# An attention and long-convolution kernel on one core: its instruction order planned with one more rule on PSUM banks

## The chip, the core and the metric

The kernel runs on one core of a Trainium2 chip. The metric is the device time of one execution in microseconds (us), the median of three runs. A core has five engines that run side by side, each in its own fixed order: TensorE (PE in the profile, its weight loads PEld), VectorE (DVE), ScalarE (ACT), GpSimd (POOL), and SyncE (SP), which here only starts transfers (DMA). Matrix products land in PSUM, which has eight banks of 512 float32 per partition; all other tiles lie in SBUF.

## The reference

Block-sparse attention, then a gated long convolution on its output. Four batches, eight heads, 768 positions, head size 64, model width 512.

```python
# attention, per batch and head
k_rep = k.reshape(B, H, 12, 64, D).mean(axis=3)          # mean key of each block of 64
gate_scores = einsum('bhsd,bhnd->bhsn', q, k_rep)        # blocks of the future: -1e9
top_idx = argsort(gate_scores)[..., -3:]                 # three best blocks, and the own one
scores = where(mask & causal, q @ k.T / sqrt(D), -1e9)
attn = softmax(scores) @ v
# hyena, per batch, x = heads side by side (768 x 512)
x1, x2, x3 = split(x @ w_proj, 3)
x2_conv = irfft(rfft(x2) * rfft(filter_fft))             # along the 768 positions
out = (x1 * x2_conv * x3) @ w_out
```

## The kernel before

The kernel works on 16 pairs of heads (`g` = 0 to 15, four pairs to a batch). Its work is first written down as a graph of 1509 small operations. Each has a tag, the engines that may run it with an assumed duration, the buffers it reads and writes, and a priority `vt`. A planner inside the kernel's source goes through the graph with a clock of its own, gives each operation an engine, a start and buffers, and sorts all operations by start. They are emitted in that order, and the framework adds the semaphores. It also makes two instructions of different engines that touch the same PSUM bank wait for each other in the order in which they were emitted.

The planner's parameters are one dictionary: offsets `v_tag` to the priority of each kind of operation, `d_tag` a handicap of VectorE where another engine may do it, `tm` the first pair whose queries are turned by DMA, `ahead` how far the planner may run in front of the attention, `warm_until` until when idle TensorE is filled with warm-up matmuls.

```python
PAR = dict(
    p0=-2.503, p1=0.149, a0=0.0, pvlag=0.364, dlag=1.728, dlen=1.178, ...
    o1=1.0, pen_dve=-0.346, ahead=3.319, delta=0.028, queue=6.537, direct=2, tm=8, kin=16, late=2.0,
    w0=1.334, wl=1.579, wlag=0.085, warm_until=31.758, tr0=-4.639, trl=2.112, fill0=-0.29, ...
)
```

The keys of a pair are transposed by TensorE into a PSUM bank, half by half. VectorE sums the bank to block means (`ks`), ScalarE or VectorE copies it to the key tile (`k2`). GpSimd splits the means into a high and a low part for the gate (`km`).

```python
def e_kt(...):  nc.tensor.transpose(E.bk(kp)[:, P*c:P*(c+1)], E.sb(kn[g])[:, HC*hf + c, :, :], E.id32)   # L368, 3 per half
def e_ks(...):  nc.vector.reduce_sum(E.sb(ks)[:, 6*hf:6*hf+6], E.bk(kp)[:, 0:HS]...)                    # L371
def e_k2(...):  (nc.scalar.copy if en == "ACT" else nc.vector.tensor_copy)(                             # L381, twice per half
                    E.sb(Kt[g])[r, HC*hf:HC*(hf+1), 1-t, :], E.bk(kp)[r, 0:HS]...)
...
def e_km(E, nc, en):
    for t in range(2):
        ...
        nc.gpsimd.tensor_copy(x[r, 2, 0:12], E.sb(ks)[r, :])                                            # L398
        nc.gpsimd.tensor_tensor(x[ru, 1, cc], E.sb(ks)[r, :], x[r, 2, 0:12], op=ALU.subtract)           # L399
        nc.gpsimd.tensor_copy(x[ru, 0, cc], x[r, 2, 0:12])                                              # L400
```

Queries take one of two ways. For pairs below `tm` TensorE transposes them (L430), ScalarE and VectorE split them (L433, L436), and after the gate (L488), the choice of blocks on VectorE (L507, L514) and a mask transpose (L536) the mask rows are copied in (L543). For pairs from `tm` on, the split is done before the turn (L458, L463), and two transposing DMAs (L468, L472) bring queries and masks to the query tile.

Attention: scores (L566), exp on ScalarE (L573), causal corner on GpSimd (L578), values (L596), normalising on VectorE (L605, L609), even and odd sums `eo` (L634, GpSimd or VectorE), a transposing DMA to `xT` (L628), and a first Fourier stage (L646, L653) copied to `XT` (L659, ScalarE or VectorE).

Hyena of a batch: products with the filter's spectrum `t` (L755, then L764 on VectorE), their sums `Y` (L774, GpSimd or VectorE), the two gates `x1` and `prod` (L791; L797 on ScalarE or VectorE, L800 on VectorE), the way back (L818), `ce` and `sd` (L827, L833), `yT` (L839, GpSimd or VectorE), output product (L849), eviction `osb` (L853, ScalarE or VectorE) and store (L856).

The planner's choice of the start of an operation and its bookkeeping, cut:

```python
def at(o, e, f):
    est = max(free[e], o.ready, f)
    if o.lock and e == "DVE":
        est = max(est, free["POOL"])
    if e == "POOL":
        est = max(est, lock_dve)
    if o.size > 200:
        est = max(est, chan - par["queue"])
    return est
...
    if e == "PE" and 0.4 <= free[e] < par["warm_until"] and (
            not cands or min(c[0] for c in cands) > free[e] + 0.1):
        cands.append((free[e], filler()))          # a warm-up matmul, L950 in the profile
```

Of the kernel before, what the change touches and what calls it, by code (L numbers as in the profile page):

```python
# [12 lines left out]
ALU = mybir.AluOpType  # L13
# [31 lines left out]
for _pi, _segs in enumerate(PIECES):  # L45
# [3 lines left out]


PAR = dict(
    p0=-2.503, p1=0.149, a0=0.0, pvlag=0.364, dlag=1.728, dlen=1.178, h0=5.163, hlen=3.776, f0=-0.278,
    f1=4.952, ld=-1.045, s2a=-0.184, s2b=0.461, x0=0.517, x1=0.943, c0=0.51, c1=0.761, o0=1.574,
    o1=1.0, pen_dve=-0.346, ahead=3.319, delta=0.028, queue=6.537, direct=2, tm=8, kin=16, late=2.0,
    w0=1.334, wl=1.579, wlag=0.085, warm_until=31.758, tr0=-4.639, trl=2.112, fill0=-0.29, v_yT=0.58, v_sd=0.159,
    d_k2=0.711, v_trig=-0.056, v_ldq=-0.072, v_max=0.214, v_g=1.014, v_Y=0.003, v_k2=-0.006, v_rec=-0.068, v_small=0.756,
    v_gate=-0.111, v_km=-0.109, d_x1=0.207, d_shQ=0.303, v_xT=-0.322, v_prod=-0.4, v_ldv=-0.291, d_yT=0.059, v_ks=0.021,
    v_osb=0.119, v_ldk=-0.647, v_kT=-0.152, v_gT=0.375, d_md=0.183, d_trig=0.402, v_qT=-0.009, v_mT=-0.03, v_lt=-0.053,
    v_fe=-0.62, d_eo=0.463, v_md=0.013, v_phase=0.942, v_shQ=0.405, v_ldf=0.502, d_Y=0.618, v_sel=-0.073, v_warm0=-0.481,
    v_x1=-0.19, v_ldw=-0.109, v_tab=-0.895, v_va=0.322, v_iota=0.312, d_XT=0.43, v_qh=0.06, v_h0=0.127, v_eblk=-1.554,  # L60
    v_id32=-0.347, v_st=0.292, v_nyq=0.459, v_s2=0.435, v_st1=0.097, v_XT=0.005, v_t=-0.034, v_ql=0.179, v_hf=0.099,
    d_g=0.166, d_ce=0.66, d_osb=-0.651, d_fill=0.096, v_w=-0.194, v_ce=-0.772, v_fill=-0.313, v_op=-0.002, v_pv=-0.131,
    d_w=0.06, v_nrm=-0.309, v_ha=-0.507, v_id16=-0.192, v_eo=0.145, v_x13=-0.234, d_fe=0.294, v_cv=0.151, v_sc=-0.043,
    v_T2=0.596, v_T1=0.196, d_qh=0.116, v_pq=-0.067, d_pq=0.376, v_ex=-0.001,
)

POOLS = dict(kn=2, qn=3, vn=2, k2=1, qx=4, ks=2, km=3, m8=2, nm=1,
# [8 lines left out]
class Buf:  # L76
    def __init__(self, pool, seq=None):
        self.pool, self.slot, self.left, self.seq = pool, None, 0, seq
        self.w, self.r = {}, {}
        self.free = self.busy = 0.0  # L80
        self.users = []


class Op:
# [4 lines left out]
class Graph:  # L89
# [3 lines left out]
    def add(self, tag, vt, eng, emit, rd=(), wr=(), res=(), lock=False, size=0):  # L93
        o = Op()
        vt += self.par.get("v_" + tag, 0.0)
        o.i, o.tag, o.vt, o.eng, o.emit, o.lock, o.size = len(self.ops), tag, vt, eng, emit, lock, size
        deps = set()

        def norm(xs):
            return [x if isinstance(x, tuple) else (x, 0) for x in xs]  # L100

        bufs = []
        for b, p in norm(rd):
            deps.update(b.w.get(p, ()))
            b.r.setdefault(p, []).append(o)
            bufs.append(b)
        for b, p in norm(wr):
            deps.update(x for x in b.w.get(p, ()))
            deps.update(x for x in b.r.get(p, ()) if x is not o)
            b.w.setdefault(p, []).append(o)  # L110
            bufs.append(b)
        deps.discard(o)
        o.deps = list(deps)
        o.bufs = list({id(b): b for b in bufs}.values())
        for b in o.bufs:
            b.left += 1
        o.alloc = list({id(b): b for b in o.bufs + list(res)}.values())
        self.ops.append(o)
        return o
# [17 lines left out]
def pol(occ):  # L137
    return occ, occ + 0.11


def build(par):
# [62 lines left out]
    def e_eblk(E, nc, en, h=0):  # L204
        x = E.eblk[64 * h:64 * h + 64, :]
        nc.gpsimd.memset(x, EMASK)
        nc.gpsimd.affine_select(out=x, in_=x, compare_op=ALU.is_ge, fill=0.0, base=0, pattern=[[1, S]],
                                channel_multiplier=-64)
        nc.gpsimd.affine_select(out=x, in_=x, compare_op=ALU.is_ge, fill=0.0, base=63, pattern=[[-1, S]],
                                channel_multiplier=64)  # L210

    for h in range(2):
        add("eblk", T0 + 3 + h, {"POOL": pol(2.2)}, lambda E, nc, en, h=h: e_eblk(E, nc, en, h), wr=[(cb("eblk"), h)])

    slot_init = []
    for i in range(POOLS["kt"]):
        def e_fq(E, nc, en, i=i):
            eng = nc.vector if en == "DVE" else nc.gpsimd
            eng.memset(E.t["qt"][i][0:64, :, 0, :], 0.0)
            eng.memset(E.t["qt"][i][64:76, 0, 1, :], 0.0)  # L220

        def e_fk(E, nc, en, i=i):
            eng = nc.vector if en == "DVE" else nc.gpsimd
            for h in range(2):
                r = slice(0, 64) if h == 0 else slice(64, 76)
                eng.tensor_copy(E.t["kt"][i][r, :, h, :], E.eblk[r, :].rearrange("p (c s) -> p c s", s=P))

        slot_init.append([
            add("fill", par["fill0"] + i, {"DVE": (0.55, 0.7), "POOL": pol(1.1)}, e_fq, wr=[cb(("slot", i))], lock=True),
            add("fill", par["fill0"] + i, {"DVE": (0.55, 0.7), "POOL": pol(1.6)}, e_fk,  # L230
                rd=[(cb("eblk"), 0), (cb("eblk"), 1)], wr=[(cb(("slot", i)), 1)], lock=True)])
    def e_small(E, nc, en):
        for t_ in E.t["km"]:
# [112 lines left out]
    def prep(g):  # L346
# [44 lines left out]
        def e_km(E, nc, en):  # L391
            x = E.sb(km)
            for t in range(2):
                r = slice(64 * t, 64 * t + 64)
                u = 1 - t if by_dma else t
                ru = slice(64 * u, 64 * u + 64)
                cc = slice(12 * u, 12 * u + 12)
                nc.gpsimd.tensor_copy(x[r, 2, 0:12], E.sb(ks)[r, :])  # L398
                nc.gpsimd.tensor_tensor(x[ru, 1, cc], E.sb(ks)[r, :], x[r, 2, 0:12], op=ALU.subtract)  # L399
                nc.gpsimd.tensor_copy(x[ru, 0, cc], x[r, 2, 0:12])  # L400

        add("km", v(.3), {"POOL": pol(1.45)}, e_km, rd=[(ks, 0), (ks, 1), cb("small")], wr=[km])

        def shuffle(src, col, dst, vt, tag):
            for t in range(2):
                def e_sh(E, nc, en, t=t):
                    r = slice(64 * t, 64 * t + 64)
                    o = E.sb(dst)[r, :, 1 - t, :]
                    i_ = E.sb(src)[r, col:col + S].rearrange("p (c s) -> p c s", s=P)
                    if en == "SP":  # L410
                        nc.sync.dma_start(o, i_)
                    else:
                        (nc.vector if en == "DVE" else nc.gpsimd).tensor_copy(o, i_)
                eng = {"DVE": dve(S, 4), "POOL": pol(0.86)} if direct else {"SP": (0.5, 0)}
                add(tag, vt, eng, e_sh, rd=[(src, 0), (src, 1)], wr=[(dst, ("h", t, 0)), (dst, ("h", t, 1))],
                    size=0 if direct else 130, lock=direct)

# [462 lines left out]
def plan(par):  # L880
# [81 lines left out]
# [5 lines that stand above are left out]
            est = max(est, lock_dve)  # L967
        if o.size > 200:
            est = max(est, chan - par["queue"])
        return est  # L970

    vt_floor = [o.vt for o in ops if o.tag == "sc"]
# [5 lines left out]
    while left:  # L978
# [29 lines left out]
        for b in o.alloc:  # L1008
            if b.pool is None or b.slot is not None:
                continue  # L1010
            s, f = slot_for(b)
            b.slot, b.free = s, f
            if b.seq is not None:
                turn[b.pool].remove(b.seq)
            kk = [("bk", i) for i in range(s, s + (2 if b.pool == "sp" else 1))] if b.pool in ("bk", "sp") else [(b.pool, s)]
            o.pre += [u for x in kk for u in last.get(x, ())]
            for x in kk:
                last[x] = b.users
            if b.pool in ("bk", "sp"):
                for i in range(s, s + (2 if b.pool == "sp" else 1)):  # L1020
                    banks[i] = None
            else:
                pools[b.pool][s] = None
# [26 lines left out]
        for s in o.succ:  # L1050
            s.ready = max(s.ready, o.done)
            s.nd -= 1
            if s.nd == 0:
                for x in s.eng:
                    ready[x].append(s)
        for b in o.bufs:
            b.left -= 1
            b.busy = max(b.busy, o.done)
            b.users.append(o)
            if b.left == 0 and b.pool is not None:  # L1060
                if b.pool in ("bk", "sp"):
                    for i in range(b.slot, b.slot + (2 if b.pool == "sp" else 1)):
                        banks[i] = b.busy
                else:
                    pools[b.pool][b.slot] = b.busy
# [91 lines left out]
```

## Time and profile before

| | |
|---|---|
| median time, three runs | 246.58 us (246.48 to 246.77) |
| span of the profiled run | 245.2 us |
| PE busy | 229.1 us, of it 17.2 warm-up matmuls (114) |
| DVE busy | 207.7 us, 642 instructions |
| ACT busy | 171.5 us, 287 instructions |
| POOL busy | 151.2 us, 304 instructions |
| mean DMA rate | 169 GB/s |

The span is a little shorter than the time, since it runs from the first to the last instruction. Busy time counts an engine while it works on an instruction; matmuls are pipelined and their ends are modelled, so TensorE can be called busy and still have small gaps. A line such as "ACT kt L381 <- DVE ks L371" in the view of waits says that ScalarE stood idle before line 381 until VectorE had done line 371; the engine that gave the last signal is named.

### The profile page before, as it was taken

The page shows a single profiled execution, that of the slowest core. Times are in us where ns is not written, and L with a number is a line of the kernel's source. Part 1 is how long each engine was busy: PE and PEld are TensorE (multiplying, and loading weights), DVE is VectorE, ACT ScalarE, POOL GpSimd, SP SyncE. Part 2 cuts the span into 40 slices and gives each one's busy share as a digit, 9 for nine tenths or more (in the row PEclk, how much of TensorE's full clock was granted, in tenths as well). Part 3 has the DMA queues.
Part 4 walks back from the last instruction along what each step waited for, and adds up shares of the span by engine and source line. Part 5 has one row for each costly group of instructions (what it writes and reads, how often), then busy time and mean ns, then how long its engine had stood idle before and what let it go on. Part 6 is the DMA issues. An engine that isn't in the chain of part 4 may idle for free.

```text
span 245.2 us, 6521 instructions
## 1 busy us (share of the span) xinstructions
PE 229.1 (93%) x2330; PEld 154.4 (63%) x2330; DVE 207.7 (85%) x642; ACT 171.5 (70%) x287; POOL 151.2 (62%) x304
## 2 busy tenths in 40 slices
PE   8998799889899999898999989999999999999993
PEld 6887476567675766555666556676666566645651
DVE  6997887878889889899989895998897878799984
ACT  3969888998989976868599558969567754314410
POOL 8867567647558984775579778847477643054010
PEclk9999999999999999999999999999999999999999
DMA  7999597879999896898999999458546301222006
GB/s 175 307 232 266 125 251 174 192 187 215 250 199 256 207 259 142 182 221 187 239 225 198 217 242 218 79 70 196 127 111 167 92 0 31 90 87 86 3 9 248
DMA packets 122304, 41.45 MB, mean 169 GB/s; under 512 B 116384, under 2 KB 116384, under 8 KB 122272
## 3 DMA queue, kind: packets, MB, share of 16 engines
q1 hardware_dynamic: 122272, 41.04, 72.2%
q8 instruction: 18, 0.29, 0.6%
q14 instruction: 14, 0.11, 0.2%
HBM read 24.64 MB, written 6.29 MB: 126 GB/s over the span
## 4 chain that ended last, share of the span: by engine, by line
PE 57%; ACT 18%; DVE 16%; issue 5%; POOL 3%; DVEq 0%; ACTq 0%; POOLq 0%
PE ps L791 12%; PE ps L566 8%; ACT ex L573 8%; PE ps L755 8%; PE ps L849 7%; ACT kt L381 7%; PE ps L950 5%; PE ps L596 4%; PE ps L818 4%; DVE ks L371 4%; PE ps L646 2%; DVE prod L800 2%; PE ps L368 2%; PE ps L488 2%; DVE sd L833 1%
## 5 line engine op out<-in xcount | busy, mean ns | idle before, releaser
L573 ACT ACTIVATE ex<-ps 128x1024 f16<-128x1024 f32 (+1 forms) x96 | 85.1, 930 | 14.5 <-PE ps L566 14.0
L578 POOL TENSOR_SCALAR_AFFINE_SELECT ex<-ex 128x256 f16<-128x256 f16 x96 | 42.3, 448 | 33.2 <-ACT ex L573 32.4
L566 PE MATMUL ps<-qt,kt 76*128 76x512 f16 (+7 forms) x256 | 48.7, 305 | 2.8 <-ACT ex L573 1.9
L791 PE MATMUL ps<-xT,wp 128*128 128x384 f16 x256 | 48.8, 326 | 0.6 <-DVE t L764 0.3
L381 ACT CAST kt<-ps 64x384 f16<-64x384 f32 x59 | 27.9, 473 | 11.5 <-DVE ks L371 6.4
L774 POOL TENSOR_TENSOR Y<-t,t 128x512 f16<-128x512 f32 (+1 forms) x22 | 27.8, 1269 | 12.9 <-DVE t L764 12.6
L566 PEld LDWEIGHTS <-kt 76*128 76x128 f16 (+1 forms) x256 | 22.9, 97 | 20.1 <-issue 5.2
L791 PEld LDWEIGHTS <-wp 128*128 128x128 f16 x256 | 24.6, 98 | 17.1 <-issue 1.5
L596 PEld LDWEIGHTS <-ex 128*128 128x128 f16 x672 | 25.6, 97 | 7.2 <-issue 3.4
L596 PE MATMUL ps<-va,ex 128*128 128x65 f16 x672 | 27.2, 193 | 2.5 <-DVE ks L371 1.5
L797 ACT CAST x<-ps 128x384 f16<-128x384 f32 x31 | 15.0, 484 | 16.8 <-PE ps L791 14.3
L849 PE MATMUL ps<-wo,yT 128*128 128x512 f16 x96 | 23.7, 379 | 1.0 <-ACT osb L853 1.0
L755 PE MATMUL ps<-wp,XT 128*128 128x512 f16 x96 | 24.0, 378 | 0.5 <-ACT XT L659 0.4
L800 DVE TENSOR_TENSOR prod<-ps,x 128x384 f32<-128x384 f32 x32 | 17.6, 552 | 6.5 <-PE ps L791 3.2
L371 DVE TENSOR_REDUCE ks<-ps 128x6 f32<-128x384 f32 x32 | 16.8, 550 | 5.5 <-ACT kt L381 4.8
L818 PE MATMUL ps<-G,Y 128*128 128x384 f16 x96 | 20.2, 326 | 0.3 <-ACT kt L381 0.3
L764 DVE TENSOR_TENSOR t<-ps,HA 128x512 f32<-128x512 f32 x24 | 16.4, 685 | 4.2 <-PE ps L755 3.9
L839 POOL TENSOR_TENSOR yT<-prod,sd 128x384 f16<-128x384 f32 x10 | 10.4, 1051 | 15.4 <-DVE prod L800 13.0
L609 DVE TENSOR_TENSOR xn<-ps,rec 128x384 f16<-128x384 f32 x32 | 17.7, 553 | 0.9
L950 PE MATMUL ps<-warm 128*128 128x256 f16 x114 | 17.2, 299 | 1.1 <-DVE warm L170 1.1
L634 POOL TENSOR_TENSOR eo<-xn 128x384 f16<-128x384 f16 x18 | 17.2, 957 | 1.1 <-DVE xn L609 0.7
L659 ACT CAST XT<-ps 128x512 f16<-128x512 f32 (+1 forms) x22 | 11.0, 511 | 9.8 <-PE ps L653 5.7
(116 smaller groups left out, 414.2 us busy)
## 6 DMA issues: line engine op xcount, KB each, us to landing
kn<-in_k_dram SPq DMA_DIRECT2D x32, 192.0 KB, 3.7
qn<-in_q_dram SPq DMA_DIRECT2D x32, 192.0 KB, 3.4
vn<-in_v_dram SPq DMA_DIRECT2D x16, 384.0 KB, 3.9
out_dram<-osb SPq DMA_DIRECT2D x24, 256.0 KB, 2.1
t<-in_moe_w_proj_dram SPq DMA_DIRECT2D x12, 256.0 KB, 4.2
t<-in_moe_filter_fft_dram SPq DMA_DIRECT2D x6, 256.0 KB, 4.9
qt<-qx SPq DMA_DIRECT2D x12, 96.0 KB, 3.3
t<-in_moe_w_out_dram SPq DMA_DIRECT2D x4, 256.0 KB, 2.9
```

The lines of the kernel that those rows point to most:

```text
L371: nc.vector.reduce_sum(E.sb(ks)[:, 6 * hf:6 * hf + 6], E.bk(kp)[:, 0:HS].rearrange("p (n t) -> p n t", t=64), axis=AX.X)
L381: (nc.scalar.copy if en == "ACT" else nc.vector.tensor_copy)(E.sb(Kt[g])[r, HC * hf:HC * (hf + 1), 1 - t, :], E.bk(kp)[r, 0:HS].rearrange( ...
L566: nc.tensor.matmul(o[:, col:col + w], lhsT=E.sb(Kt[g])[0:KR[t], kc, 1 - t, :], rhs=E.sb(Qt[g])[0:KR[t], q0 // P:(q0 + w) // P, 1 - t, :], ...
L573: nc.scalar.activation(E.sb(ex)[:, 0:w], E.sp(sp)[:, 0:w], AF.Exp, scale=ESC)
L578: nc.gpsimd.affine_select(out=dv, in_=dv, compare_op=ALU.is_ge, fill=0.0, base=0, pattern=[[0, 2], [1, P]], channel_multiplier=-1)
L596: nc.tensor.matmul(o[:, 65 * c:65 * c + 65], lhsT=E.sb(exs[pi])[:, col:col + P], rhs=E.sb(va[g])[:, t, kc, :], start=(kc == 0), stop=(kc = ...
L755: nc.tensor.matmul(E.bk(xa), lhsT=w, rhs=E.wp[:, j, Dm:2 * Dm], start=(j == 0), stop=(j == NP - 1))
L774: (nc.vector if en == "DVE" else nc.gpsimd).tensor_tensor(E.sb(Y)[ro, n_, :], E.sb(x)[ri, :], E.sb(y)[ri, :], op=op)
L791: nc.tensor.matmul(E.bk(xq)[:, 0:HS], lhsT=E.wp[:, d2, 2 * Dm * m + P * dc:2 * Dm * m + P * (dc + 1)], rhs=E.sb(xT[gs[d2]])[:, cs], start= ...
L818: nc.tensor.matmul(E.bk(cv)[:, 0:HS], lhsT=E.sb(Y)[:, 3 * p_ + n_, P * dc:P * (dc + 1)], rhs=E.G[:, 3 * p_ + n_, :], start=(n_ == 0), stop ...
L849: nc.tensor.matmul(E.bk(op_), lhsT=E.sb(yT)[:, d2, P * c:P * (c + 1)], rhs=E.wo[:, d2, :], start=(d2 == 0), stop=(d2 == NP - 1))
L950: nc.tensor.matmul(E.ps[:, 3584:3840], lhsT=E.warm[:, 0:P], rhs=E.warm[:, 0:256], start=True, stop=True)
```

## The change

It has four parts.

1. The planner knows that two engines do not read one PSUM bank at once: it keeps the last user of each bank buffer, and an operation on another engine starts after it is done. The order of instructions in which the semaphores are set is then the order that was planned.
2. `tm` goes from 8 to 9: the queries of the ninth pair are transposed by TensorE, and those of the tenth and later pairs by DMA.
3. For the pairs whose queries TensorE transposes, `km` writes the high part where it is needed and leaves out one copy per head: two GpSimd instructions fewer per pair.
4. Some assumed durations of setup steps are longer, and all parameters were chosen anew for the planner with this rule. Engines, order and buffers of most operations change with them.

```diff
 PAR = dict(
-    o1=1.0, pen_dve=-0.346, ahead=3.319, delta=0.028, queue=6.537, direct=2, tm=8, kin=16, late=2.0,
-    w0=1.334, wl=1.579, wlag=0.085, warm_until=31.758, tr0=-4.639, trl=2.112, fill0=-0.29, ...
+    direct=2, tm=9, kin=16, p0=-2.58, p1=0.359, pvlag=-1.081, dlag=1.538, dlen=1.485, h0=4.836,
+    ..., ahead=16.341, delta=0.011, queue=6.283, w0=1.608, wl=1.643, wlag=-7.304, warm_until=34.129, ...
     (all other parameters are new as well; cut)
 )
 ...
-        self.users = []
+        self.users, self.last, self.pre = [], None, []
 ...
-        add("eblk", ..., {"POOL": pol(2.2)}, ...)
+        add("eblk", ..., {"POOL": pol(2.48)}, ...)
 ...
-                nc.gpsimd.tensor_copy(x[r, 2, 0:12], E.sb(ks)[r, :])
-                nc.gpsimd.tensor_tensor(x[ru, 1, cc], E.sb(ks)[r, :], x[r, 2, 0:12], op=ALU.subtract)
-                nc.gpsimd.tensor_copy(x[ru, 0, cc], x[r, 2, 0:12])
-        add("km", v(.3), {"POOL": pol(1.45)}, ...)
+                hi = x[r, 2, 0:12] if by_dma else x[r, 0, cc]
+                nc.gpsimd.tensor_copy(hi, E.sb(ks)[r, :])
+                nc.gpsimd.tensor_tensor(x[ru, 1, cc], E.sb(ks)[r, :], hi, op=ALU.subtract)
+                if by_dma:
+                    nc.gpsimd.tensor_copy(x[ru, 0, cc], hi)
+        add("km", v(.3), {"POOL": pol(1.45 if by_dma else 0.96)}, ...)
 ...
         if o.size > 200:
             est = max(est, chan - par["queue"])
+        for b in o.bufs:
+            if b.last is not None and b.last.on != e:
+                est = max(est, b.last.done)
         return est
 ...
         for b in o.bufs:
+            o.pre += b.pre
+            if b.pool in ("bk", "sp"):
+                if b.last is not None and b.last.on != e:
+                    o.pre.append(b.last)
+                b.last = o
```

More of the change, by code (lines that the diff above doesn't have):

```diff
@@ L51 @@
 PAR = dict(
-    p0=-2.503, p1=0.149, a0=0.0, pvlag=0.364, dlag=1.728, dlen=1.178, h0=5.163, hlen=3.776, f0=-0.278,
-    f1=4.952, ld=-1.045, s2a=-0.184, s2b=0.461, x0=0.517, x1=0.943, c0=0.51, c1=0.761, o0=1.574,
-    o1=1.0, pen_dve=-0.346, ahead=3.319, delta=0.028, queue=6.537, direct=2, tm=8, kin=16, late=2.0,
-    w0=1.334, wl=1.579, wlag=0.085, warm_until=31.758, tr0=-4.639, trl=2.112, fill0=-0.29, v_yT=0.58, v_sd=0.159,
-    d_k2=0.711, v_trig=-0.056, v_ldq=-0.072, v_max=0.214, v_g=1.014, v_Y=0.003, v_k2=-0.006, v_rec=-0.068, v_small=0.756,
@@ L57 @@
[L57 to L61, printed above, removed]
@@ L62 @@
-    d_g=0.166, d_ce=0.66, d_osb=-0.651, d_fill=0.096, v_w=-0.194, v_ce=-0.772, v_fill=-0.313, v_op=-0.002, v_pv=-0.131,
-    d_w=0.06, v_nrm=-0.309, v_ha=-0.507, v_id16=-0.192, v_eo=0.145, v_x13=-0.234, d_fe=0.294, v_cv=0.151, v_sc=-0.043,
-    v_T2=0.596, v_T1=0.196, d_qh=0.116, v_pq=-0.067, d_pq=0.376, v_ex=-0.001,
+    direct=2, tm=9, kin=16, p0=-2.58, p1=0.359, pvlag=-1.081, dlag=1.538, dlen=1.485, h0=4.836,
+    hlen=3.401, f0=-0.546, f1=4.97, ld=-1.042, s2a=-0.355, s2b=0.464, x0=0.446, x1=1.137, c0=0.817,
@@ new lines @@
+    c1=1.054, o0=1.347, ahead=16.341, delta=0.011, queue=6.283, w0=1.608, wl=1.643, wlag=-7.304, warm_until=34.129,
+    tr0=-26.33, trl=16.468, fill0=1.323, v_yT=1.15, v_sd=-2.381, d_k2=3.845, v_trig=4.775, v_ldq=-0.068, v_max=-6.527,
+    v_g=2.311, v_Y=0.82, v_k2=0.404, v_rec=-2.613, v_small=3.535, v_gate=-0.028, v_km=1.623, d_x1=-0.346, d_shQ=0.734,
+    v_xT=-2.135, v_prod=-3.254, v_ldv=-0.43, d_yT=0.279, v_ks=0.928, v_osb=-3.052, v_ldk=-0.329, v_kT=0.038, v_gT=3.039,
+    d_md=0.144, d_trig=0.482, v_qT=0.017, v_mT=-0.085, v_lt=-3.096, v_fe=1.769, d_eo=0.005, v_md=0.045, v_phase=-0.03,
@@ new lines @@
+    v_shQ=2.489, v_ldf=0.595, d_Y=5.668, v_sel=-5.514, v_warm0=3.241, v_x1=-0.983, v_ldw=-0.146, v_tab=6.693, v_va=1.68,
+    v_iota=-1.707, d_XT=-0.476, v_qh=0.233, v_h0=0.611, v_eblk=4.461, v_id32=1.695, v_st=2.959, v_nyq=-2.837, v_s2=0.062,
+    v_st1=0.023, v_XT=0.064, v_t=-9.103, v_ql=1.449, v_hf=0.158, d_g=6.58, d_ce=8.444, d_osb=2.444, d_fill=0.427,
+    v_w=-0.555, v_ce=-1.909, v_fill=-0.339, v_op=1.026, v_pv=-1.989, d_w=4.395, v_nrm=-0.253, v_ha=-5.02, v_id16=-0.109,
+    v_eo=1.933, v_x13=-0.231, d_fe=-4.145, v_cv=-1.548, v_sc=0.113, v_T2=-0.349, v_T1=2.226, d_qh=2.343, v_pq=-4.162,
@@ L65 @@
+    d_pq=6.99, v_ex=0.251, a0=0.0, o1=1.0, pen_dve=0.205, late=2.0,
 )
@@ L212, in build @@
     for h in range(2):
-        add("eblk", T0 + 3 + h, {"POOL": pol(2.2)}, lambda E, nc, en, h=h: e_eblk(E, nc, en, h), wr=[(cb("eblk"), h)])
+        add("eblk", T0 + 3 + h, {"POOL": pol(2.48)}, lambda E, nc, en, h=h: e_eblk(E, nc, en, h), wr=[(cb("eblk"), h)])
     slot_init = []
@@ L228, in build @@
         slot_init.append([
-            add("fill", par["fill0"] + i, {"DVE": (0.55, 0.7), "POOL": pol(1.1)}, e_fq, wr=[cb(("slot", i))], lock=True),
-            add("fill", par["fill0"] + i, {"DVE": (0.55, 0.7), "POOL": pol(1.6)}, e_fk,
+            add("fill", par["fill0"] + i, {"DVE": (0.74, 0.85), "POOL": pol(1.2)}, e_fq, wr=[cb(("slot", i))], lock=True),
+            add("fill", par["fill0"] + i, {"DVE": (0.7, 0.85), "POOL": pol(1.6)}, e_fk,
                 rd=[(cb("eblk"), 0), (cb("eblk"), 1)], wr=[(cb(("slot", i)), 1)], lock=True)])
@@ L397, in e_km @@
                 cc = slice(12 * u, 12 * u + 12)
-                nc.gpsimd.tensor_copy(x[r, 2, 0:12], E.sb(ks)[r, :])
-                nc.gpsimd.tensor_tensor(x[ru, 1, cc], E.sb(ks)[r, :], x[r, 2, 0:12], op=ALU.subtract)
-                nc.gpsimd.tensor_copy(x[ru, 0, cc], x[r, 2, 0:12])
-        add("km", v(.3), {"POOL": pol(1.45)}, e_km, rd=[(ks, 0), (ks, 1), cb("small")], wr=[km])
+                hi = x[r, 2, 0:12] if by_dma else x[r, 0, cc]
[3 more added lines that the diff above has]
+                    nc.gpsimd.tensor_copy(x[ru, 0, cc], hi)
+        add("km", v(.3), {"POOL": pol(1.45 if by_dma else 0.96)}, e_km, rd=[(ks, 0), (ks, 1), cb("small")], wr=[km])
         def shuffle(src, col, dst, vt, tag):
@@ L413, in e_sh @@
                         (nc.vector if en == "DVE" else nc.gpsimd).tensor_copy(o, i_)
-                eng = {"DVE": dve(S, 4), "POOL": pol(0.86)} if direct else {"SP": (0.5, 0)}
+                eng = {"DVE": (0.37, 0.5), "POOL": pol(0.86)} if direct else {"SP": (0.5, 0)}
                 add(tag, vt, eng, e_sh, rd=[(src, 0), (src, 1)], wr=[(dst, ("h", t, 0)), (dst, ("h", t, 1))],
@@ L1015, in plan @@
             kk = [("bk", i) for i in range(s, s + (2 if b.pool == "sp" else 1))] if b.pool in ("bk", "sp") else [(b.pool, s)]
-            o.pre += [u for x in kk for u in last.get(x, ())]
+            b.pre = [u for x in kk for u in last.get(x, ())]
             for x in kk:
```

## The prediction

> **What bounds the kernel now.** I read three views in this order: busy time by engine, the same engines by stretches of the span, and the waits inside the stretch where TensorE is not full. First the page's busy shares and its forty slices (each slice is 6.1 us, each digit tenths of a slice).
>
> ```profile
> PE 229.1 (93%) x2330; PEld 154.4 (63%) x2330; DVE 207.7 (85%) x642; ACT 171.5 (70%) x287; POOL 151.2 (62%) x304
> PE   8998799889899999898999989999999999999993
> DVE  6997887878889889899989895998897878799984
> ACT  3969888998989976868599558969567754314410
> ```
>
> TensorE (PE) is the bound over the whole; VectorE (DVE) is close behind. ScalarE (ACT) is dense in the first third and empty in the last. The busy time by stretches (TensorE, weight loads, VectorE, ScalarE, GpSimd) shows where TensorE still has room:
>
> ```profile
> 0.00:34.40 34.40, 30.88 (x299) 24.07 (x300) 28.24 (x114) 26.57 (x49) 24.84 (x52) 1.00 0.91 220
> 34.40:80.00 45.60, 41.51 (x535) 30.08 (x534) 38.28 (x140) 41.58 (x70) 31.11 (x78) 1.00 0.91 215
> 80.00:121.00 41.00, 37.88 (x388) 25.25 (x387) 36.81 (x112) 30.14 (x55) 28.61 (x59) 1.00 0.88 202
> 121.00:150.00 29.00, 27.60 (x280) 18.04 (x278) 25.19 (x73) 21.86 (x35) 22.82 (x42) 1.00 1.15 226
> 150.00:240.00 90.00, 89.79 (x833) 56.52 (x831) 77.34 (x205) 51.36 (x83) 43.82 (x75) 1.00 0.37 89
> 240.00:245.20 5.20, 1.41 (x7) 0.45 (x5) 1.80 (x3) 0.00 (x0) 0.00 (x0) 1.00 0.61 226
> ```
>
> TensorE idles 3.5, 4.1, 3.1, 1.4, 0.2 and 3.8 us in these six stretches, 16.1 in all. From 150 us on it is full: nothing a new order does there can pay, apart from the last 3.8 us (last eviction and store). Before 34.4 us most of its work is warm-up: the group of "warm" matmuls is 17.2 us of the 229.1. So TensorE's own work is 211.9 us, and the span is 211.9 + 17.2 + 16.1.
>
> Between 34 and 121 us these waits stand on the path of keys (columns: total, times, longest):
>
> ```profile
> ACT kt L381 <- DVE ks L371: 4.6, 6, 1.2
> DVE ks L371 <- ACT kt L381: 3.5, 7, 0.9
> PE ps L596 <- DVE ks L371: 1.5, 2, 0.8
> PEld ps L430 <- ACT kt L381: 1.2, 2, 0.7
> PE ps L596 <- ACT kt L381: 0.9, 1, 0.9
> ```
>
> L371 sums a transposed key bank, L381 copies the same bank. Neither reads what the other writes, so no data explains why each waits for the other. The timeline shows the pattern once: sums, copies 0.66 us late, TensorE 0.70 us late behind the copies.
>
> ```profile
> 25.03 1.00 DVE L371 TENSOR_REDUCE ks<-ps 128x6 f32<-128x384 f32 x2
> 25.60 1.94 ACT L381 CAST kt<-ps 64x384 f16<-64x384 f32 x4 [0.66 <-DVE ks L371]
> 26.61 0.55 PE L430 MATMUL ps<-id,qn 128*128 128x128 f32 x3 [0.70 <-ACT kt L381]
> ```
>
> The copies of the first half start when the first sum (0.5 us) is done, not with it. The old order was planned as if both read together.
>
> **What the Trainium skill says.** "PSUM — Partial Sum Buffer", section "PSUM bank collisions raise a hardware error": two engines on one bank and the same 32 partitions at once is an error, two reads included, and software has to keep them apart. The trace agrees as far as it can: the two readers come one after the other, with the waits above. So the rule costs nothing new on the chip; the waits are there already, and the change only tells the planner. "TensorE: Matmul & The Clock Gate", section "Wait — 56ns, not 53.3ns?": back-to-back warm matmuls start 215.7 ns apart at 512 columns. The trace has 24 output matmuls in 5.19 us at the end of the chain of waits, 216 ns each: the late stretch runs at the array's rate. "GPSIMD Engine Reference", section "1. Specifications": GpSimd's SBUF interfaces are shared with VectorE, which can contend. The trace shows a hint: L399 usually takes 0.21 us and once 1.19.
>
> **The change part by part**, counted in the built order of both kernels, durations from the rows of the kernel before.
>
> *Queries of the ninth pair go back to TensorE.* Plus 6 float32 transposes at 7.3/48 = 0.152 us and 5 mask transposes at 3.5/40 = 0.088: +1.35 us of TensorE. One pair of DMA transposes goes and two small copies come; they lie beside other work.
>
> *GpSimd steps.* 9 pairs lose two copies each, 18 x 0.192 = 3.5 us. GpSimd is 62% busy, so alone this only shortens the way to the gate by 0.4 us per pair.
>
> *The new order moves work off VectorE.* All 24 output evictions are on ScalarE (18 fewer here, 18 x 0.683 = 12.3); the half-height Y products leave (8 x 0.947 = 7.6), 13 yT products (13 x 0.598 = 7.8), 6 weight casts (2.5), 5 key copies (2.8), 3 query copies (2.5), and small ones (about 3.6). In come 15 XT copies (5 x 0.413 + 10 x 0.682 = 8.9), 16 x1 copies (8.7), 4 eo and 2 Y (3.5). Net about -18 us, 207.7 to 190. ScalarE changes by +2 (18 x 0.586 in, XT and x1 out), GpSimd by +22 (13 x 1.051 yT, 8 x 1.265 Y, minus what left), to about 174. None is on TensorE, so this pays only as shorter waits.
>
> *Warm-up.* 143 warm matmuls in place of 114. 25 in a row took 2.89 us, so 29 x 0.116 = +3.4 us of TensorE. They stand where the planner now sees waits; part takes the place of idle time that is there already. The first stretch has 3.5 us of it, of which 1.1 are the start; I let 1.5 be replaced. 110 of them now stand before the first score, 86 before.
>
> *The middle.* Before, TensorE idles 4.1 + 3.1 + 1.4 = 8.6 us between 34.4 and 150. There is some more in its busy time: at full rate the columns of its own work add up to about 208.3 us, 3.5 below 211.9. So 12.1 us are to be had. In 34.4 to 80 ScalarE is 91% busy, and idle 4.0. Up to the 37th exp the new order gives it about as much work from the first exp on (58.0 us by these durations, 57.2 before), so it can only gain the waits, 2 to 3 us. Key copies tell why: before, ScalarE had 7 runs of four copies in a row and 11 of two; now 3 of four and 20 of two, with exps between, which is how a bank busy with the sum is filled over. In 80 to 150 TensorE's work was lumpy: 37 us of it between the 37th and 49th exp, 25 and 18 in the next two dozens. Now it is 27, 26, 27. ScalarE stood without an exp from 105 to 121 us; that gap should close, and VectorE, 90% busy there, has less to do. I take the 12.1 down to 4.9, that is -7.2. How much of it goes is the choice in this sum.
>
> Sum: 1.35 + 3.4 - 1.5 - 7.2 = -4.0 us. The span was 245.2 and the median time 246.58, so 246.58 - 4.0 = 242.6; I say 242.5.
>
> **Rivals.** (1) *Nothing gained*: the warm-up costs its 4.8 us with the added transposes, and the bank waits were hidden behind a ScalarE that is 91% busy anyway. Then the middle gives 3 or 4 back and the time stays at 246 to 248. For it: the order before ran TensorE at 93%; ScalarE's work before the 37th exp grows by 2.7 us. Against it: waits of 8.1 us between L371 and L381 from 34 to 121 us. (2) *GpSimd and VectorE become the bound.* From the 37th to the 85th exp the new order asks 103 us of TensorE, 98 of VectorE, 90 of GpSimd; in-order engines so evenly loaded stall each other, and GpSimd's yT takes 1.05 us where VectorE took 0.60. Then 247 to 250. For it: the GpSimd sum. Against it: POOL was free in the second half, and the last four yT still are on VectorE. (3) *The plan fits the chip*: with the rule and longer setup costs in it, hardly a wait stays in the middle, -10 or -11 there: 238 to 239. For it: from 150 us on the old plan already ran without a gap, where hardly any bank is read by two engines.
>
> **Range and chances.** Rival 3 gives the lower end and some more for early idle: 236. Rivals 1 and 2 give the upper: 249. 2% faster is 241.65, hardly below my middle, so faster and same are equal: 0.45 each, slower 0.10.
>
> **What would show it.** VectorE near 190 us, GpSimd near 174; the warm group at 143; TensorE idle under 5 us between 34 and 150; waits between L371 and L381 under half of 11.2 us (6.4 and 4.8 on the whole); the 37th exp starting at 78 to 81 us (79.3 before, in the timeline). Wrong would be: the first score later than 23 us (19.9 before) without a shorter middle, new waits for GpSimd's yT or Y on TensorE's path, or waits of Q transposes for DMA.

## The result, and the profile after

The changed kernel takes 235.82 us (235.32 to 236.36, 4 runs) beside 246.68 us for the kernel before in the same runs: ratio 0.956, 95% interval 0.9536 to 0.9583, that is 10.9 us less. The prediction was 242.5 us with a range from 236 to 249. Faster was right; the gain was 2.7 times the predicted one, and the time lies just below the range.

The page's busy shares and slices of the kernel after (a slice is now 5.9 us):

```profile
PE 227.7 (97%) x2370; PEld 157.6 (67%) x2370; DVE 193.7 (83%) x617; ACT 174.6 (75%) x288; POOL 170.9 (73%) x312
PE   8998999999999999999999999999999999999993
DVE  6688988888799999899898889888996887596850
ACT  3989999999989889897967886967575656304243
```

The eights in the middle of the TensorE row are gone. The stretches, in the same columns as before (the last 5.2 us are again a stretch of their own):

```profile
0.00:34.40 34.40, 32.52 (x334) 26.85 (x335) 28.08 (x110) 28.88 (x55) 26.73 (x55) 1.00 0.99 240
34.40:80.00 45.60, 44.72 (x575) 32.69 (x572) 39.80 (x140) 44.54 (x73) 32.12 (x66) 1.00 0.95 224
80.00:121.00 41.00, 41.00 (x456) 28.84 (x455) 37.40 (x133) 34.91 (x58) 35.86 (x72) 1.00 0.99 213
121.00:150.00 29.00, 29.00 (x314) 19.80 (x313) 26.35 (x78) 22.88 (x37) 26.59 (x48) 1.00 1.04 220
150.00:229.00 79.00, 78.95 (x697) 48.96 (x696) 62.04 (x160) 41.84 (x67) 49.58 (x74) 1.00 0.29 79
229.00:234.20 5.20, 1.47 (x7) 0.49 (x5) 0.00 (x0) 1.54 (x3) 0.00 (x0) 1.00 0.58 217
```

TensorE idles 1.9, 0.9, 0, 0, 0.05 and 3.7 us, 6.5 in all in place of 16.1. Its busy time hides a second gain, since a matmul counts as busy until its modelled end, while the next one may start long before. So I count from start to start. In both traces like matmuls in a row start 215 ns apart at 512 columns, 162 at 384, 108 at 256, 55 at 128 (109 in float32), 29 at 65 and 25 at 24. With these distances TensorE's own matmuls add up to 202.7 us before and 203.6 after. What their starts are further apart than that, beyond the idle time, are hidden gaps: 11.3 us before, 5.5 after. The warm-ups (114, now 143) take 15.1 and 18.5 us from start to start, the first two dozen or so at 213 ns each.

The account closes: idle -9.62, hidden gaps -5.78, warm-up +3.45, added transposes +0.93, together -11.02, as the span (245.24 to 234.22).

The waits between key sums and key copies from 34 to 121 us, those for TensorE's transposes ahead of them:

```profile
ACT kt L381 <- PE ps L368: 2.3, 4, 1.5
...
DVE ks L371 <- ACT kt L381: 0.6, 2, 0.4
ACT kt L381 <- DVE ks L371: 0.6, 1, 0.6
```

4.6 and 3.5 us have become 0.6 and 0.6, and no line of TensorE waits there for a key sum. How a bank's readers now stand apart is seen in the timeline of one pair:

```profile
44.54 0.55 DVE L371 TENSOR_REDUCE ks<-ps 128x6 f32<-128x384 f32 x1
45.04 1.07 ACT L575 ACTIVATE ex<-ps 128x1024 f16<-128x1024 f32 x1
45.95 0.97 ACT L381 CAST kt<-ps 64x384 f16<-64x384 f32 x2
46.82 0.56 DVE L371 TENSOR_REDUCE ks<-ps 128x6 f32<-128x384 f32 x1
46.94 1.62 ACT L575 ACTIVATE ex<-ps 128x1024 f16<-128x1024 f32 x2
48.45 0.47 ACT L381 CAST kt<-ps 64x384 f16<-64x384 f32 x1
```

VectorE sums the first half until 45.09. ScalarE does an exp and copies the half from 45.95 on. While VectorE sums the second half, ScalarE does two exps, and copies that half from 48.45 on. No idle time stands ahead of any of these lines. The chain that ended last, before and after, says the same of the whole:

```profile
PE 57%; ACT 18%; DVE 16%; issue 5%; POOL 3%; DVEq 0%; ACTq 0%; POOLq 0%
PE 81%; ACT 8%; DVE 7%; issue 3%; ACTq 0%; DVEq 0%
```

### The profile page after: what moved, and what is told of

Read it like the earlier page. It is cut to its first block, busy times and chain, and to the rows that moved or that the text cites. A ratio compares the mean times of both kernels' runs of the same rounds, so it can differ in the third digit from the quotient of the medians.

```text
span 234.2 us, 6574 instructions
## 1 busy us (share of the span) xinstructions
PE 227.7 (97%) x2370; PEld 157.6 (67%) x2370; DVE 193.7 (83%) x617; ACT 174.6 (75%) x288; POOL 170.9 (73%) x312
## 4 chain that ended last, share of the span: by engine, by line
PE 81%; ACT 8%; DVE 7%; issue 3%; ACTq 0%; DVEq 0%
PE ps L793 18%; PE ps L568 12%; PE ps L851 9%; PE ps L757 8%; PE ps L598 8%; PE ps L820 7%; PE ps L952 5%; PE ps L368 4%; PE ps L648 4%; ACT ex L575 3%; PE ps L490 3%; ACT kt L381 2%; PE ps L655 2%; DVE qx L438 1%; PE ps L432 1%
## 5 line engine op out<-in xcount | busy, mean ns | idle before, releaser
L580 POOL TENSOR_SCALAR_AFFINE_SELECT ex<-ex 128x256 f16<-128x256 f16 x96 | 42.8, 452 | 22.5 <-ACT ex L575 20.5
L568 PE MATMUL ps<-qt,kt 76*128 76x512 f16 (+7 forms) x256 | 49.8, 305 | 0.3
L776 POOL TENSOR_TENSOR Y<-t,t 128x512 f16<-128x512 f32 (+1 forms) x32 | 40.5, 1272 | 11.9 <-DVE t L766 10.9
L381 ACT CAST kt<-ps 64x384 f16<-64x384 f32 x64 | 30.3, 474 | 10.1 <-PE ps L368 8.2
L855 ACT COPY osb<-ps 128x512 f32<-128x512 f32 x24 | 14.1, 589 | 16.9 <-PE ps L851 16.8
L841 POOL TENSOR_TENSOR yT<-prod,sd 128x384 f16<-128x384 f32 x23 | 23.3, 1024 | 4.0 <-DVE prod L802 2.6
L757 PE MATMUL ps<-wp,XT 128*128 128x512 f16 x96 | 23.2, 379 | 0.2 <-ACT kt L381 0.2
L952 PE MATMUL ps<-warm 128*128 128x256 f16 x143 | 20.7, 292 | 1.1 <-DVE warm L170 1.1
L371 DVE TENSOR_REDUCE ks<-ps 128x6 f32<-128x384 f32 x32 | 17.3, 549 | 2.4 <-ACT kt L381 1.9
L820 PE MATMUL ps<-G,Y 128*128 128x384 f16 x96 | 18.2, 326 | 0.0
L835 DVE TENSOR_TENSOR sd<-ce,ps 128x384 f32<-128x384 f32 x32 | 16.1, 550 | 2.0 <-ACT ce L829 1.3
L952 PEld LDWEIGHTS <-warm 128*128 128x128 f16 x143 | 14.7, 105 | 4.1 <-DVE warm L170 1.1
```

Source lines behind the costliest of these rows:

```text
L381: (nc.scalar.copy if en == "ACT" else nc.vector.tensor_copy)(E.sb(Kt[g])[r, HC * hf:HC * (hf + 1), 1 - t, :], E.bk(kp)[r, 0:HS].rearrange( ...
L568: nc.tensor.matmul(o[:, col:col + w], lhsT=E.sb(Kt[g])[0:KR[t], kc, 1 - t, :], rhs=E.sb(Qt[g])[0:KR[t], q0 // P:(q0 + w) // P, 1 - t, :], ...
L580: nc.gpsimd.affine_select(out=dv, in_=dv, compare_op=ALU.is_ge, fill=0.0, base=0, pattern=[[0, 2], [1, P]], channel_multiplier=-1)
L757: nc.tensor.matmul(E.bk(xa), lhsT=w, rhs=E.wp[:, j, Dm:2 * Dm], start=(j == 0), stop=(j == NP - 1))
L776: (nc.vector if en == "DVE" else nc.gpsimd).tensor_tensor(E.sb(Y)[ro, n_, :], E.sb(x)[ri, :], E.sb(y)[ri, :], op=op)
L820: nc.tensor.matmul(E.bk(cv)[:, 0:HS], lhsT=E.sb(Y)[:, 3 * p_ + n_, P * dc:P * (dc + 1)], rhs=E.G[:, 3 * p_ + n_, :], start=(n_ == 0), stop ...
```

## The experiments

Theory A: the old order lost its time to bank waits that its planner did not know of. Its rival B: the gain came from new parameters, which spread the hyena work and lighten VectorE. Later two more were needed: C, parameters fit one order alone, and E, rule and parameters only work together. "Idle" below is TensorE's idle time from 34.4 to 150 us: 8.6 before, 0.9 after.

### One half of the change at a time

```diff
 # e1_rule_only: the kernel before, and (keeping of b.last cut)
+        for b in o.bufs:
+            if b.last is not None and b.last.on != e:
+                est = max(est, b.last.done)
```

> The kernel before with the bank rule in its planner and nothing else: old parameters, old query turn, old GpSimd steps. Theory A (the old order lost its time to bank waits that its planner did not know of; telling it is most of the gain): 238 to 241 us, TensorE idle between 34 and 150 us down from 8.6 to under 4. Theory B (the gain is in the newly chosen parameters, which spread the hyena work and lighten VectorE; the rule alone just makes another order): 244 to 249 us, idle still 7 or more.

Measured: 244.57 us, ratio 0.992 (0.990 to 0.995), idle 6.5. In part this run had a lower clock; columns of the two stretches as above, the clock is the third number from the end:

```profile
15.00:20.00 5.00, 3.48 (x45) 3.01 (x46) 4.91 (x12) 4.31 (x11) 1.68 (x3) 0.85 1.16 263
20.00:25.00 5.00, 5.00 (x33) 3.41 (x32) 4.30 (x21) 4.50 (x10) 2.81 (x9) 0.81 1.06 239
```

At 0.85 and 0.81 for 5 us each, at most 5 x 0.15 + 5 x 0.19 = 1.7 us of TensorE's speed was lost. Even without that the rule alone falls short of A.

But the trace shows that the rule took the bank waits away, and where part of the gain was lost. Over the whole span the waits between L371 and L381 fell from 11.2 us to 0.2. The first exp, though, starts 5.3 us later (before, and this run):

```profile
23.00 1.94 ACT L573 ACTIVATE ex<-ps 128x1024 f16<-128x1024 f32 x2
28.30 1.94 ACT L573 ACTIVATE ex<-ps 128x1024 f16<-128x1024 f32 x2
```

With the rule the old parameters put more setup work, mask copies and key copies of ScalarE ahead of it. (The clock is not the reason: in e15, below, the first exp starts at 28.6 us with a mean clock of 0.999.) Of the 5.3 us, 2.9 hold work of TensorE's own that had stood later, by the distances above, and 2.4 are lost. From the first exp on, the time in which TensorE does no work of its own is 22.5 us in place of 26.2: 3.7 won there.

```diff
 # e2_no_rule: the kernel after, and
-            if b.last is not None and b.last.on != e:
-                est = max(est, b.last.done)
```

> The changed kernel with the rule alone taken out of its planner, new parameters kept; the semaphores still keep two readers of a bank apart. Theory A: bank waits come back, 240 to 246 us, waits between the key sums and key copies over 8 us in all (3.1 with the rule). Theory B: 234 to 238 us, since engines and spread stay much as they are.

Measured: 247.3 us, ratio 1.003 (1.002 to 1.004), idle 8.2, just above A's range; the waits between sums and copies are 6.8 us, under the 8 of A. New engines, new spread and a lighter VectorE (195.6 us) are all there, and the gain is gone. So B falls: without the rule the new parameters make the kernel no faster. A falls as well in its plain form, since the rule alone gives 2 us.

### What the shared key bank costs

```diff
 # e3, e4: the sums read loaded keys in SBUF
-    E.bk(kp)[:, 0:HS].rearrange("p (n t) -> p n t", t=64)
+    E.sb(kn[g])[:, HC*hf:HC*(hf+1), :, :].rearrange("p c t d -> p (c t) d")
```

> The kernel before, its order kept, but the key sums read a float32 SBUF tile of the same size in place of the PSUM bank: sums of other numbers, so other blocks are chosen, with the same work. It takes away the sharing of the bank between sum and copy. Theory A: the waits between the two lines vanish and the time falls by 4 to 8 us, to 239 to 243. Theory B: these waits were hidden beside a full ScalarE or in an order that stalls anyway, 244.5 to 246.5 us.

> The same replacement in the changed kernel, its order kept. Both theories: little is left to gain, 235 to 236 us, as TensorE idles only 0.9 us between 34 and 150. If it fell by over 1.5 us, bank waits would still cost in the new order.

Measured: 244.5 us (ratio 0.990, 0.988 to 0.993) and 242.2 us (0.981, 0.978 to 0.984). Both leave out the true block means. They decide little, for the edit brought a wait of its own (in e3 the two runs at a mean clock of 1.00 took 242.5 and 242.7 us, the nine others 243.8 to 246.9 at lower clocks). These are waits from 15 to 34 us in the changed kernel with this edit (its lines after L371 have numbers one higher):

```profile
PE ps L539 <- DVE nm L522: 3.2, 1, 3.2
...
DVE ks L371 <- DMA kn<-in_k_dram: 3.1, 1, 3.1
```

VectorE waits for keys to land, and TensorE stands behind VectorE. Presumably the next keys were loaded later because the late sums held one of only two key buffers. So the edit was made again with a tile that nobody loads:

```diff
 # e5, e6, e7: the sums read the constant identity, three times over
+    bass.AP(tensor=x_.tensor, offset=x_.offset, ap=[[x_.ap[0][0], P], [0, 3], [64, 2], [1, 64]])
```

This too leaves out the true means; the number of elements is the same. It also takes away the sums' wait for the transposes, but in the kernel before the sums had never idled for TensorE (their releasers were the copies with 4.8 us and GpSimd with 0.6).

> The kernel before, order kept, the key sums read a constant SBUF tile of the same number of float32 (the identity, read three times over), so that sum and copy share no bank and no buffer of loaded keys is held longer. It leaves out the true block means, with the same work. Theory A (bank waits unknown to the planner cost the old order its time): 239 to 243 us, TensorE idle between 34 and 150 us under 5 (8.6 before). Theory B (the waits are hidden; the gain came from the new spread of work): 244.5 to 247 us.

Measured: 239.78 us, ratio 0.973 (0.971 to 0.975), idle 4.9.

```profile
34.40:80.00 45.60, 44.03 (x574) 32.22 (x573) 40.79 (x158) 43.90 (x73) 34.01 (x81) 1.00 0.96 223
80.00:121.00 41.00, 38.95 (x393) 25.99 (x391) 37.41 (x103) 32.02 (x55) 29.39 (x66) 1.00 0.98 221
```

Against the kernel before, TensorE's idle time in the first of these stretches fell from 4.1 to 1.6 us and in the second from 3.1 to 2.0. With no other change the old order is 6.7 us faster when sum and copy don't meet in a bank. The waits that the profile named are a true cost, of the size of six tenths of the gain; the first exp alone comes 1.6 us earlier (21.4 us in place of 23.0). The edit also frees the bank without the sum, so the sum's and the copies' own waits are not told apart.

> The new parameters without the rule in the planner (247.3 us), order kept, and the key sums read the constant SBUF tile, so that the chip is what this planner believed it to be as far as the key banks go. Theory A: most of the 11.5 us come back, 236 to 240 us. Theory C (the parameters were found for one order only; any other order of the planner is worse whatever the waits): 244 to 247 us.

Measured: 243.76 us, ratio 0.990 (0.988 to 0.991), idle 6.1. Only 3.5 of 11.5 us came back. An order planned without the rule is not good even where the key banks are no longer shared. Other banks with two readers remain (the mask copies L545 are on both engines now), and which part they have was not tried.

> The changed kernel, order kept, with the key sums from the constant tile. All theories: 234.5 to 236 us, since its bank waits are 3.1 us in sum and none stands before TensorE. More than 1.5 us off would say that bank waits still cost in the new order.

Measured: 234.67 us, ratio 0.953 (0.951 to 0.954), idle 0.7. Some 0.8 us below the changed kernel by the ratios: the shared bank costs the new order next to nothing.

### Parts of the new order

```diff
 # e8_osb_dve: the kernel after, order kept
+                en = "DVE" if b < B - 1 else en       # 18 output evictions
```

> The changed kernel, order kept, with the output evictions of the first three batches (18 of 24) on VectorE again, at 0.68 us each in place of ScalarE's 0.59. VectorE back to about 206 us. If the lighter VectorE is a cause of the gain: 239 us or more, TensorE idle between 34 and 150 us over 3. If it only follows from the plan and does not limit: 236 to 237.5 us.

Measured: 239.4 us, ratio 0.972 (0.970 to 0.973): 3.6 us lost, idle 1.9. VectorE is at 203.3 us.

```profile
80.00:121.00 41.00, 40.48 (x449) 28.14 (x447) 38.11 (x134) 32.16 (x53) 34.96 (x71) 1.00 1.02 222
121.00:150.00 29.00, 28.52 (x288) 18.85 (x288) 25.87 (x78) 20.69 (x33) 26.35 (x46) 1.00 0.99 209
```

Only 1.0 us of it is TensorE's new idle time in these stretches; more lies in gaps inside its busy time (229.4 in place of 227.7) and after 150 us. The idle time is below the 3 us that were forecast, the time is not. So the lighter VectorE does count in this order, if not by itself (e2); an order planned with these evictions on VectorE was not tried.

```diff
 # e9_fewer_warm: every fourth warm-up after the first 16 isn't emitted (31 fewer; counting cut)
+                if n_warm > 16 and n_warm % 4 == 0:
+                    continue
```

> The changed kernel, order kept, without every fourth warm-up matmul after the first 16 (112 left of 143). If each stands before work that is ready, as the prediction had it: 31 x 0.116 = 3.6 us less, 232 us. If they stand in gaps that are there anyway: 235 to 236. If the clock of TensorE falls for want of them: 237 to 240, with a granted clock below 1.

Measured: 235.7 us, ratio 0.958 (0.954 to 0.962). The first stretch, whole and for the warm-ups alone:

```profile
0.00:34.40 34.40, 29.64 (x314) 23.34 (x315) 28.54 (x110) 29.12 (x56) 26.80 (x55) 1.00 0.96 232
0.00:34.40 34.40, 16.59 (x110) 11.26 (x110) 1.00 0.96 232
```

TensorE is busy 2.9 us less than with all warm-ups, and the kernel isn't faster: the removed ones left idle time in their place. These 31 stand in gaps. The clock stayed at 1.00 in this stretch of the profiled run; over the whole kernel two of the four runs had a mean of 0.993, and one of these took 237.9 us.

```diff
 # e10_tm8
-    direct=2, tm=9, ...
+    direct=2, tm=8, ...
```

> The changed kernel with the ninth pair's queries turned by DMA as before; the planner makes a new order with the same parameters. By its own cost (1.35 us less on TensorE): 234.5 us. If parameters fit one order alone: 238 to 245 us with TensorE idle between 34 and 150 us over 3.

Measured: 241.66 us, ratio 0.980 (0.979 to 0.982), idle 5.8. The removed transposes would be about 1 us less; the new order that the planner makes costs over 5. What the query turn is worth by itself can't be read from this.

```diff
 # e11_old_km: the kernel after, order kept, three steps for every pair
-                hi = x[r, 2, 0:12] if by_dma else x[r, 0, cc]
+                hi = x[r, 2, 0:12]
-                if by_dma:
-                    nc.gpsimd.tensor_copy(x[ru, 0, cc], hi)
+                nc.gpsimd.tensor_copy(x[ru, 0, cc], hi)
```

> The changed kernel, order kept, with the three GpSimd steps per head of before for the nine pairs that had lost one, 18 copies of 0.19 us. As a part of its own: within 0.5 us of the changed kernel, 235.5 to 236.5 us, as GpSimd is 73% busy and nothing on TensorE waits for it.

Measured: 236.25 us, ratio 0.958 (0.957 to 0.960), against 0.956 (0.954 to 0.958): the fewer GpSimd steps are worth 0.4 us at the most likely, and the intervals overlap.

### Neighbours of both orders

```diff
 # e12_jitter: h0=4.836 -> 4.9    e17_new_rule_a: h0=4.836 -> 4.79    e18_new_rule_b: hlen=3.401 -> 3.44
 # e13, e14: the kernel before, h0=5.163 -> 5.2, 5.12;  e15, e16: the same with the rule
```

> The changed kernel with one parameter moved a little: the start of the hyena stage from 4.836 to 4.9 pairs. All parts of the change stay. If the rule and the parts make the gain: 235 to 237.5 us. If the gain is one order that the search found: 238 to 242 us.

> The changed kernel with the start of its hyena stage at 4.79 in place of 4.836. If the shifted order at 242.0 us was bad luck: 235 to 238. If the order on record is a narrow best: 239 to 243.

> The changed kernel with the length of its hyena stage at 3.44 in place of 3.401. If the shifted order at 242.0 us was bad luck: 235 to 238. If the order on record is a narrow best: 239 to 243.

> The kernel before with the start of the hyena stage moved from 5.163 to 5.2 pairs, no rule. Theory A (the rule as such gives better orders, whatever the parameters): 247 to 252 us, clearly above its neighbour with the rule. Theory E (parameters and order are found together; the rule only lets the search see what the chip does): 247 to 252 as well, but no better with the rule.

> The kernel before with the start of the hyena stage at 5.12 pairs, no rule. Both theories: 247 to 252 us.

> Old parameters with the start at 5.2 and the rule in the planner. Theory A: 2 us or more below its neighbour without the rule. Theory E: within 1.5 us of it or above.

> Old parameters with the start at 5.12 and the rule. Theory A: 2 us or more below its neighbour without the rule. Theory E: within 1.5 us of it or above.

The last two columns are from the profiled run: the time without own work of TensorE, ahead of the first exp and from there to the end. It is the stretch less TensorE's own matmuls by the distances above, so idle time, hidden gaps and warm-ups together.

| parameters | planner | us (ratio to before, interval) | idle | ahead | from there |
|---|---|---|---|---|---|
| old, shifted to 5.2 (e13) | no rule | 246.9 (1.000, 1.000 to 1.001) | 8.3 | 16.2 | 26.4 |
| old, shifted to 5.12 (e14) | no rule | 249.4 (1.011, 0.999 to 1.022) | 10.9 | 15.9 | 30.2 |
| old, shifted to 5.2 (e15) | rule | 244.6 (0.991, 0.989 to 0.994) | 6.8 | 19.0 | 21.1 |
| old, shifted to 5.12 (e16) | rule | 249.0 (1.009, 1.006 to 1.012) | 8.4 | 18.6 | 25.7 |
| new, start 4.9 (e12) | rule | 242.0 (0.982, 0.981 to 0.984) | 2.9 | 16.1 | 20.4 |
| new, start 4.79 (e17) | rule | 239.0 (0.970, 0.967 to 0.972) | 2.6 | 16.5 | 17.2 |
| new, length 3.44 (e18) | rule | 241.8 (0.981, 0.978 to 0.984) | 4.2 | 16.9 | 19.8 |

The profiled run of e16 had a mean granted clock of 0.979, that of e14 0.993, so their times are not all order. Old parameters without the rule give 246.6 to 249.4 us; with it 244.6 (e1), 244.6 and 249.0: two of three 2 us better, one the same. A's "2 us or more" holds for e15; for e16 it does not show in the time, and with two runs each, three of the four at clocks of 0.979 to 0.993, that stays open. New parameters with the rule give 239.0 to 242.0 with small shifts, and 241.7 with the older query turn. The kernel on record, with 235.8, is 3 to 6 us better than any of them. In the order of e12:

```profile
80.00:121.00 41.00, 39.18 (x438) 27.16 (x436) 37.34 (x130) 33.84 (x58) 32.09 (x71) 1.00 1.00 210
121.00:150.00 29.00, 28.80 (x289) 18.98 (x288) 26.34 (x78) 20.29 (x31) 23.60 (x38) 1.00 1.04 201
```

it idles 1.8 and 0.2 us where the order on record idles not at all; with 2.2 us more idle after 150, 0.3 more in the first stretch and 1.5 more of busy time that makes up its 6.0 us. Parts and rule are the same, and the parameters but for one. The planner gives engines differently too: VectorE is at 199.4 us and GpSimd at 162.0 in e12, 193.7 and 170.9 on record. VectorE's load is not all of it: e17 has 193.8 us there and still takes 239.0. So the gain divides about like this: from 246.6 to about 241 us (the mean of e10, e12, e17 and e18 is 241.1) by rule and new parameters together, and another 5 us by this one order.

Divided at the first exp, rule and parameters can be told apart. From there on, the rule takes off 3.7 us (before to e1), 5.3 (e13 to e15) and 4.5 (e14 to e16) with old parameters; with new ones the 24.5 us of e2 become 17.2 to 20.7 in the neighbours and 13.8 on record. With old parameters the rule costs 2.4 to 2.8 us ahead of the first exp (16.3 us before, 18.7 in e1), with the new ones nothing (17.0 in e2, 16.8 on record). So the rule pays some 4 to 7 us behind the first exp with either parameters. The new parameters pay 2 to 4 us more there in the neighbours and spare the loss at the start; this one order adds the rest. Which of the new parameters do this was not tried, nor were the longer assumed durations of part 4 by themselves.

## Why the prediction was right or wrong

*What bounds the kernel, and that the bank waits are a true cost*: right. e5 gives them 6.7 us in the old order, and in the changed kernel the waits between L371 and L381 are 3.1 us over the whole span in place of 11.2. Rival 1, that they are hidden behind a full ScalarE, is refuted by it.

*Engines*: right. VectorE was put near 190 us and measured 193.7, GpSimd near 174 (170.9), ScalarE +2 (+3.1). Rival 2 did not come: from 80 to 150 us TensorE is without idle time beside a VectorE that is 91% busy. But e8 shows how near it is: 9.6 us more on VectorE cost 3.6 us.

*Queries and GpSimd steps*: small, as said. The steps alone are within 0.5 us (e11). From start to start the added transposes are 0.9 us, not 1.35; the query turn by itself was not measured.

*Warm-up, +3.4 - 1.5*: right as an account (+3.4 from start to start, first stretch -1.6 of idle), wrong as a cost. By e9, 31 of them take no time that TensorE could use. The first exp starts at 23.10 us where it had started at 23.00, although the first score came at 22.2 in place of 19.9. From about 19 us on ScalarE goes in both traces without idle time from its copies and query splits into a table load of 1.28 us (at 21.71 us before, 21.81 after) and from it into the first exp. So it is ScalarE's own order that ends last there; no run changes it by itself.

*The middle*: here the prediction failed, in the step "I take the 12.1 down to 4.9, that is -7.2". The term measured -7.7 of idle time from 34 to 150 us and -5.8 of hidden gaps over the span (-3.9 of it from 34 to 150), -13.5 in all. Two things in it were mis-sized. The room was too small: the 208.3 us "at full rate" are 202.7 by the distances in the trace, so 11.3 us were hidden and not 3.5. (The same subtraction after shows that 208.3 was too high: 227.7 - 20.7 = 207.0 us of busy time without the warm-ups, the added transposes included.) And I let 40% of the room stay, where 0.9 us of idle time stayed. The limit set for 34 to 80 us, where ScalarE was to gain 2 to 3 us, was about right: its idle time there fell from 4.0 to 1.1 us. The 37th exp starts at 77.1 us, below the 78 to 81 I had said, and at 78.9 before, where I had read 79.3. What I underrated is 80 to 150 us, where 4.5 us of idle time fell to none.

*Why so far off*: 242.5 us is about what neighbours of this order take (239.0 to 242.0). My sum used how much work each engine has, and a share of the room guessed on top; how well one order fits was not in it, and that is worth some 5 us. Rival 3 (238 to 239, "the plan fits the chip") was the right story and still too small. By the sum's own terms a middle without any gap would have been 246.58 - 12.1 + 1.35 + 3.4 - 1.5 = 237.7 us, and the range went 1.7 below that. The measured time got past it mainly because the hidden gaps were larger than my estimate: 5.8 us went where I had 3.5, against the 0.9 of idle time that stayed.

*Still open*: what makes this order fit. It is not chance on the chip: the planner's own clock, worked out from the source of each kernel and not measured, ends at 229.8 us for this order and at 234.1 to 236.9 for e10, e12, e17 and e18, so most of the difference was planned. With the rule this clock ends 2 to 7 us before the measured span, with old parameters and no rule 10 to 14 us before it. That the neighbours wait for readers of other shared banks was not tried.

## What to carry to other kernels

A planner's model of waits and its parameters belong together: the missing rule could not be bought with parameters (247.3 us), and of what the rule alone (244.6) won behind the first exp, more than half was lost again ahead of it. So divide a trace at a landmark before you say that a rule did little. When a bound engine is at 93% and its idle time lies in the middle, let the range reach down to an order without gaps, and count the gaps that its busy time hides as well; the work of each engine doesn't say how well an order fits. And before crediting an order's gain to a part of the change, shift one harmless parameter: here that cost 3 to 6 of 11 us.

## What the runs showed of the hardware

A lower clock of TensorE came with stretches in which it stood. In e4 it was busy 2.2 of the 5 us from 20 to 25 us, with a granted clock of 0.70 there and 0.62 in the next 5 us. In e1, busy 3.5 of 5 us from 15 to 20 us, it was 0.85 and then 0.81. In e14, 2.8 of 5 us from 90 to 95 were followed by 0.67; but 3.0 of 5 us from 105 to 110 in the same run left it at 1.00. A quarter fewer warm-ups (e9) left it at 1.00 in the first 34 us. With GpSimd busier, the split of queries on VectorE from SBUF (L463, now L465; 8 and 7 times) took 1118 ns in the mean in place of 908, the shortest about the same (816 and 784); whether GpSimd is the cause was not tried. The one long L399 that the prediction named (GpSimd, 1188 ns at 168.9 us, usually 205 to 208) had such a split beside it, from 169.2 us for 804 ns.
